# Filter work moved in a fused Fourier-mixing and SwiGLU kernel: additions behind both products, negations into the next step

## The chip, the cores and the metric

The kernel runs on one core of a Trainium2 chip. The metric is the device time of one execution in microseconds (us). Before the change four runs took 2838.94 to 2840.62 us, with a median of 2839.59 us. One more execution, which the hardware profiler recorded, took 2840.11 us; the span from its first to its last instruction is 2838.3 us.

## What is computed

```python
X = np.fft.rfft(x, axis=1)               # x: 8 batches, 3008 tokens, 256 channels
Y = X * (filt_r + 1j * filt_i)[None]     # one complex filter for all batches
y = np.fft.irfft(Y, n=3008, axis=1)
t = y.reshape(8 * 3008, 256)
g = t @ w_gate                           # 256 -> 1536
out = (g * (1 / (1 + np.exp(-g))) * (t @ w_val)) @ w_out     # 1536 -> 256
```

All of it is in float32.

## The kernel before

**Stages.** The Fourier transform of 3008 = 47 x 64 points is done as small matrix products in several stages with DRAM between them, and the two-layer network behind it uses products saved by algebra: four blocks of the input are combined into sums, so that fewer products are needed and the results are put together by additions. A batch goes through the network in 12 steps: 4 chunks of tokens (k) by 3 groups of hidden columns (g), step = 3k + g. While batch b is in the network, the transform of batch b+1 is done in pieces between its matmuls: steps 0 to 3 hold the first transform stage ("quads", L679), steps 4 to 10 the middle stages ("fours", L739), and the last stage (stage3, L919) is spread over several steps. Batch 0's transform is a prologue of about 78 us, batch 1's is done in batch 0's steps by other code, and batch 7's steps have no next transform.

**The order is written by hand.** SCHEDULE (L87 to L95) is a list of tokens that every step is issued from (loop at L1382), and pin() keeps each engine's instructions in that order. A token is one piece of work on one or two engines. Q, P, A, B and E are products on TensorE (L1034), W are the products with w_out (L1131). On ScalarE are f (negated copy of a product, L1049), c (copy, L1053), m (L1069), g and u (SiLU, L1076), and those s and e whose pair is listed with an x or a y token (L1060, L1065): they fill a PSUM bank from SBUF before a product adds to it. On VectorE are x and y, the other s and e, which fill a bank directly (L1056, L333 is the helper that records most of these), l (L329), h and v (L1081), o (L326) and z (L1102). On GpSimd are D (L1051, recorded at L329), S (sums of hidden tiles, L1085) and n (combined inputs of the next chunk). A prime marks work of the step before. A t token goes on with a last-stage piece. A b token, of which there are eight in a step (b0 to b7), goes on with the quads or the fours.

**Fours.** Step 4 + w handles part w of the filter (w = 0 to 5). Its generator yields seven times: at b0 the matmuls, b1 to b3 the evictions and the product of the transform with the real part of the filter (L779), b4 a DMA that swaps real and imaginary rows into tile q. At b5 VectorE multiplies the first half of q by the imaginary part (L818) and GpSimd adds it to y (L820, recorded at L326); at b6 the same for the second half; at b7 the filter's tile is given back and part w+1 is loaded. All these tiles are slices of one tile, lent. The products of step 5 + w's b0 read y.

**The filter.** The fours read the filter from one prepared array in DRAM (f_dram). Batch 1 builds it in its steps 0 to 2, at the tokens in FILTER_AT (L102; the code at L1413). At f1, P0, Q2 and h0 a DMA copies a piece of a filter from DRAM to DRAM (keep_filter). For the rows that need a minus sign, negated_filter(w, stage) works on one sixth of the imaginary filter: stage 0 is four DMAs into SBUF (L318), stage 1 a multiplication by -1 on ScalarE (L321, 64 x 1024), stage 2 one DMA out (L323). A step does two sixths: stage 0 at c1 and g0, stage 1 at u13 and E23, stage 2 at u01 and n1. Even sixths use one slice of lent, odd ones another.

**Queues.** Almost all DMAs are issued by SyncE's queue (SP), in program order; ScalarE issues the stores of the quads' and fours' results (d<-lent) between its own work. wt_t is the network's weights, of which four pieces are loaded again in every step from batch 1 on (L477), t is the last stage's input (L668), lent<-in_x_dram the next batch's input (L621).

Of the kernel before, what the change touches and what calls it, by code (L numbers as in the profile page):

```python
# [88 lines left out]
t4.3' W1 i3 x4.o' S10' x03 S11' i4 s13 b3 x5.o' P1 i5 o1 b4 t0.2 P0 o2 i6 z0.o c1 i7 D01 A13 g1 c0  # L89
i8 S20' Q2 S21' g0 y01 m13 t1.0 h0 i9 f2 s01 W6 t1.1 h1 i10 x23 D02 P2 o6 D12 A01 i11 c2 B13 g2 n3'  # L90
m01 t0.3 S30' t1.2 x02 W7 S31' g13 y12 y02 B01 h13 o7 t1.3 t2.0 s02 s12 g01 h2 b5 Q3 t2.1 h01 e12
A02 y23 b6 W4 e02 y03 m02 g3 A12 o4 z2.o t2.2 E12 m12 B02 t2.3 l12 b7 E02 u12 e13 g02 t3.0 h3 s23
l02 B12 v12 E13 t3.1 h02 u02 A23 n2 l13 g12 v02 W5 s03 e23 h12 e01 m23 A03 o5 z3.o u13 E23 t3.2 m03
v13 E01 l23 e03 t3.3 t4.0 l01 u23 B23 v23 u01 t4.1 E03 n1 v01 g23 B03 l03 W3 h23 g03 u03 h03 v03
""".split()  # L95
# [3 lines left out]
S00 S01 W1 S20 S21 S10 S11 W5 o1 W2 o5 S30 S31 W6 o2 z0.o o6 W3 o3 z1.o x0.o x1.o x2.o x3.o x4.o  # L99
x5.o W7 q4 o7 z3.o W4 o4 z2.o X0.o X1.o X2.o X3.o X4.o X5.o  # L100
""".split()
FILTER_AT = ("f1", "P0", "Q2", "h0", "c1", "g0", "u13", "E23", "u01", "n1")  # L102
BLOCKS = (0, 1, 3, 2)
PAIRS = ((0, 1), (1, 2), (2, 3), (0, 2), (1, 3), (0, 3))
PAIRS_USED = ((1, 3), (0, 1), (0, 2), (1, 2), (2, 3), (0, 3))
# [98 lines left out]
def kernel(  # L204
# [10 lines left out]
    nc = tc.nc  # L215
# [97 lines left out]
    def negated_filter(w, stage):  # L313

        t = room_of("et"[w % 2])[0:64].rearrange("p (s c) -> p s c", c=C)
        if stage == 0:
            for q in range(4):
                pin(nc.sync.dma_start(out=t[16 * q:16 * q + 16],  # L318
                                      in_=filter_rows(1, q // 2, q % 2, 4 * w, 4)))
        elif stage == 1:  # L320
            pin(nc.scalar.mul(t, t, -1.0))  # L321
        else:
            pin(nc.sync.dma_start(out=f_pairs[:, 0, 1, 4 * w:4 * w + 4], in_=t))  # L323

    def add(eng, dst, a, b):
        return eng.tensor_tensor(out=dst, in0=a, in1=b, op=ALU.add)  # L326
# [254 lines left out]
    class Spectral:  # L581
# [157 lines left out]
        def fours(self, w):  # L739

            tb = self.tb.pop(w)
            home, there = [], []
            if w:
                home = [bank(f"qc_{self.b}_{w}_{e}") for e in range(2)]
                y = self.p.pop(w - 1)
                for s in (0, 2, 1, 3):
                    for e in range(2):
                        r = slice(64 * e, 64 * e + 64)
                        pin(nc.tensor.matmul(  # L749
                            out=home[e][s // 2 * 64:s // 2 * 64 + 64, s % 2 * C:s % 2 * C + C],  # L750
                            lhsT=tb[r, 1, 64 * s:64 * s + 64], rhs=y[r, s],
                            start=s % 2 == 0, stop=True, skip_group_check=True))
            if w < N_FOUR:
                t = self.t2.pop(w)
                there = [bank(f"qb_{self.b}_{w}_{p}") for p in range(2)]
                for s in range(2):
                    for e in range(2):
                        for p in range(2):
                            r = slice(64 * p, 64 * p + 64)
                            a = 64 * (2 * s + e)  # L760
                            pin(nc.tensor.matmul(  # L761
                                out=there[p][64 * e:64 * e + 64, ts(s, C)],
                                lhsT=tb[r, 0, a:a + 64], rhs=t[r, s, e],
                                start=s == 0, stop=True, skip_group_check=True))
            yield
            z = y = None
            raw = []
            if w < N_FOUR:
                y = self.p[w] = room_of("y").rearrange("p (s c) -> p s c", c=C)
                there = [t.rearrange("p (s c) -> p s c", c=C) for t in there]  # L770

            def keep(p):
                t = t1pool.tile([128, NV, C], FP32, name=f"raw_{self.b}_{w}_{p}", tag="t1", bufs=2)
                raw.append(t)
                pin(nc.scalar.copy(out=t, in_=there[p]))

            def real(p):
                a = slice(2 * p, 2 * p + 2)
                pin(nc.vector.tensor_tensor(out=y[:, a], in0=there[p], in1=self.f[w][:, 0, a],  # L779
                                            op=ALU.mult))  # L780

            if home:
                z = room_of("g").rearrange("p (h f) -> p h f", h=2)
                pin(nc.scalar.copy(out=z[:, 0], in_=home[0]))
                pin(sub(nc.vector, z[:, 1], z[:, 0], home[1]))
            if there:
                keep(0)
            yield
            if home:
                pin(add(nc.vector, z[:, 0], z[:, 0], home[1]))  # L790
            if there:
                keep(1)
                real(0)
            yield
            if there:
                real(1)
            if home:
                rows = self.d2_tokens.rearrange("(h n) (r s) c -> (n r) h (s c)", h=2, r=2)
                for p in range(2):
                    at = (4 * w - 4 + 2 * p) * C  # L800
                    pin(nc.scalar.dma_start(out=rows[:, :, at:at + 2 * C],
                                            in_=z[64 * p:64 * p + 64]))
            yield
            q = None
            if there:
                q = room_of("e").rearrange("p (s c) -> p s c", c=C)
                for p in range(2):
                    pairs = [t.rearrange("(q r) s c -> q r s c", r=2)
                             for t in (q[:, 2 * p:2 * p + 2], raw[p])]
                    for r in range(2):  # L810
                        self.load(out=pairs[0][:, r], in_=pairs[1][:, 1 - r])
                self.load_four(w + 1)
            self.load_turns(w + 1)
            yield
            for half in range(2):
                a = slice(2 * half, 2 * half + 2)
                if there:
                    pin(nc.vector.tensor_tensor(out=q[:, a], in0=q[:, a], in1=self.f[w][:, 1, a],  # L818
                                                op=ALU.mult))
                    pin(add(nc.gpsimd, y[:, a], y[:, a], q[:, a]))  # L820
                yield
            if there:
                self.f.pop(w)
            self.load_filter(w + 1)
# [336 lines left out]
    with tc.tile_pool(name="start", bufs=1) as spool0:  # L1161
# [12 lines left out]
        n = 0  # L1174
# [154 lines left out]
    for b in range(B):  # L1329
# [35 lines left out]
        for step in range(NCHUNK * NG + (b == B - 1)):  # L1365
# [16 lines left out]
            for place, token in enumerate(SCHEDULE):  # L1382
                if b == 0 and this and place * TICKS % len(SCHEDULE) < TICKS and \
                        (step or place > SCHEDULE.index("A01")):
                    preparation.tick(step)
                old = token.endswith("'")
                op = token.rstrip("'")
                if op[0] == "i":
                    if older is not None and older.b == 0:
                        older.project(op)  # L1390
                elif op[0] == "t":
                    n = int(op[1])
                    ps = pieces_before if old else pieces
                    if n < len(ps):
                        next(ps[n], None)
                elif op[0] == "b":
                    next(bursts[step] if this else gap, None)
                elif op[0] in "Wo" or op.endswith(".o"):

                    g0 = older if old else before  # L1400
                    if g0 is not None and (old or not ghost):
                        g0.project(op)
                else:
                    g0 = before if old else this
                    if g0 is not None and not (ghost and op[0] == "S"):
                        g0.step(op)
                if old or this is None:
                    continue
                if b == 0 and (step, op) == (5, "A23"):
                    nxt.load_two(0)  # L1410
                if b + 2 < B and (step, op) in ((11, "Q2"), (11, "B01")):
                    following.load_x(int(op == "B01"))
                if b == 1 and step < 3 and op in FILTER_AT:  # L1413
                    n = FILTER_AT.index(op)
                    if n < 4:
                        keep_filter(4 * step + n)
                    else:
                        negated_filter(2 * step + n % 2, n // 2 - 2)
                if b and chunk and op == "B01":
                    cur.load_t4(chunk, 1)  # L1420
                for i in range(2):
                    if nxt and (step, op) == (10, ("A12", "E23")[i] if b else "E23"):
                        nxt.load_t4(0, i)
                for f, args in chores.get((step, op), ()) if b == 0 else ():
                    f(*args)
                if op in ends and not last and (b or step >= NT * NG - 1):
                    reload_weights((g + 1) % NG, ends[op])
# [34 lines left out]
```

## Time and profile before

| | |
|---|---|
| profiled execution | 2840.11 us |
| its span | 2838.3 us |
| median of four runs | 2839.59 us |
| matmuls busy | 2789.4 us, 98% of the span |
| weight loads busy | 2316.3 us, 82% |
| VectorE, ScalarE, GpSimd busy | 72%, 55%, 54% |
| negations L321 | 6, 1046 to 1057 ns each, from 474.8 to 536.6 us |
| products L818 | 72, 678 to 1603 ns each, median 865 ns |
| additions of 128 x 512 on GpSimd | 84, mean 1273 ns |
| steps of batch 1 | begin at 451.33, 480.54, 510.65, 542.66 us, and so on |

A float32 matmul is two records here, and in full flow the starts of two 128 x 188 matmuls are 159 ns apart although each is listed with some 322 ns, so busy shares of TensorE overlap. In a group's line the number behind the bar is busy time and mean duration, and then the idle time of the engine ahead of these instructions with what ended it. A timeline line gives start, duration, engine, source line, operation and count; what is in square brackets is the idle time before it and its releaser. A step begins where its first product (Q0, wk) does.

### The profile page before, as it was taken

How to read it: one execution, taken by the hardware profiler on the slowest of the kernel's cores; microseconds unless marked ns; L12 is line 12 of the kernel's file. 1: busy time of each engine (PE TensorE's matmuls, PEld its weight loads, DVE VectorE, ACT ScalarE, POOL GpSimd, SP SyncE). 2: the span in 40 equal slices, each digit the busy share in tenths (PEclk: the TensorE clock that was granted, in tenths of full speed). 3: DMA queues.
4: the chain of work that ended last, by engine and by line, in shares of the span. 5: the costliest groups of instructions: out<-in, count | busy, mean ns of one | idle time of the engine just before them, and what ended most of it. 6: DMA issues, size and time to landing. Idle time of an engine off the chain costs nothing.

```text
span 2838.3 us, 48561 instructions
## 1 busy us (share of the span) xinstructions
PE 2789.4 (98%) x15432; PEld 2316.3 (82%) x15432; DVE 2034.2 (72%) x4603; ACT 1566.7 (55%) x4202; POOL 1525.1 (54%) x1671
## 2 busy tenths in 40 slices
PE   8999999999999999999999999999999999999998
PEld 6777878788888888888888888878888888888887
DVE  6898766677667777677767677667776767766666
ACT  6775445555555555555555555555555555555554
POOL 4886566454545554455543555444554454545543
PEclk9999999999999999999999999999999999999999
DMA  9687867877666775667666676667765677645443
GB/s 231 221 269 250 274 204 226 271 222 231 189 186 203 246 219 177 199 212 235 218 182 199 212 237 205 188 190 233 229 204 177 214 221 227 195 146 153 151 137 82
DMA packets 363372, 586.58 MB, mean 207 GB/s; under 512 B 198388, under 2 KB 246260, under 8 KB 363024
## 3 DMA queue, kind: packets, MB, share of 16 engines
q1 hardware_dynamic: 337922, 534.73, 60.1%
q10 hardware_dynamic: 23406, 45.43, 5.9%
q0 software_dynamic: 1792, 3.34, 0.5%
q8 instruction: 125, 2.05, 0.3%
q14 instruction: 127, 1.04, 0.1%
HBM read 467.87 MB, written 101.34 MB: 201 GB/s over the span
## 4 chain that ended last, share of the span: by engine, by line
PE 86%; DVE 4%; POOL 3%; issue 2%; DMA 1%; ACT 0%; SPq 0%; POOLq 0%; DVEq 0%; ACTq 0%
PE wa L1034 23%; PE wk L1034 16%; PE wA L1131 16%; PE we L1034 12%; PE wG L1131 8%; PE wF L1131 4%; PE pd L937 3%; PE wqa L690 2%; PE wqc L749 1%; PE wqb L761 1%; DMA lent<-in_filt_i_dram 1%; DVE lent L818 1%; DVE y L333 1%; POOL out_dram L1116 1%; POOL h L329 0%
## 5 line engine op out<-in xcount | busy, mean ns | idle before, releaser
L1034 PE MATMUL wa<-y_t,wt_t 128*128 128x188 f32 x4464 | 880.9, 323 | 6.1 <-DVE wa L1056 2.0
L1034 PEld LDWEIGHTS wa<-y_t,wt_t 128*128 128x128 f32 x4464 | 747.1, 190 | 84.1 <-ACT wa L1060 11.0
L1034 PEld LDWEIGHTS wk<-y,wt_t 128*128 128x128 f32 x2976 | 494.7, 190 | 106.1 <-issue 33.4
L1034 PE MATMUL wk<-y,wt_t 128*128 128x188 f32 x2976 | 571.3, 325 | 0.0
L329 POOL TENSOR_TENSOR h<-h 128x376 f32<-128x376 f32 x572 | 557.9, 998 | 15.4 <-DVE h L326 15.2
L326 POOL TENSOR_TENSOR h<-h 128x376 f32<-128x376 f32 x190 | 183.6, 987 | 708.8 <-DVE h L1081 708.8
L1131 PE MATMUL wA<-h,wo_t 128*128 128x376 f32 x1532 | 551.3, 482 | 4.2 <-DVE o L326 4.1
L1034 PE MATMUL we<-y_t,wt_t 128*128 128x188 f32 x2232 | 435.2, 324 | 8.0 <-DVE we L333 4.1
L329 POOL TENSOR_TENSOR D<-f,f 128x376 f32<-128x376 f32 x288 | 280.0, 987 | 254.9 <-ACT f L1049 254.8
L329 DVE TENSOR_TENSOR we<-we,m 128x376 f32<-128x376 f32 x576 | 318.6, 554 | 121.5 <-PE we L1034 63.8
L1034 PEld LDWEIGHTS we<-y_t,wt_t 128*128 128x128 f32 x2232 | 369.3, 190 | 13.9 <-DVE we L333 8.2
L1131 PEld LDWEIGHTS wA<-h,wo_t 128*128 128x128 f32 x1532 | 274.8, 190 | 114.8 <-issue 11.1
L1069 ACT COPY m<-wa 128x376 f32<-128x376 f32 x576 | 272.8, 474 | 85.6 <-PE wa L1034 82.6
L333 DVE SCALAR_TENSOR_TENSOR y<-wk,c 128x376 f32<-128x376 f32 x480 | 246.3, 539 | 57.4 <-ACT c L1053 36.0
L1076 ACT ACTIVATE g<-wa 128x188 f32<-128x188 f32 x576 | 187.9, 326 | 165.1 <-PE wa L1034 154.9
L1131 PE MATMUL wG<-h,wo_t 128*128 128x376 f32 x768 | 274.3, 480 | 0.0
L1076 ACT ACTIVATE u<-we 128x188 f32<-128x188 f32 x576 | 188.3, 328 | 153.9 <-DVE we L329 147.7
L1053 ACT COPY c<-wk 128x376 f32<-128x376 f32 x288 | 136.4, 474 | 224.8 <-PE wk L1034 200.7
L1049 ACT ACTIVATE f<-wk 128x376 f32<-128x376 f32 x288 | 140.5, 488 | 174.0 <-PE wk L1034 142.2
L1065 ACT COPY we<-y 128x376 f32<-128x376 f32 x480 | 221.8, 480 | 18.4 <-DVE h L1081 13.7
L1081 DVE TENSOR_TENSOR h<-wa,g 128x188 f32<-128x188 f32 x576 | 198.6, 345 | 33.7 <-ACT g L1076 33.5
L1081 DVE TENSOR_TENSOR h<-we,u 128x188 f32<-128x188 f32 x576 | 197.4, 344 | 30.8 <-ACT u L1076 20.0
(162 smaller groups left out, 3516.7 us busy)
## 6 DMA issues: line engine op xcount, KB each, us to landing
wt_t<-w_all SPq DMA_DIRECT2D x174, 896.0 KB, 4.7
wt_t<-w_all SPq DMA_DIRECT2D x174, 768.0 KB, 4.4
lent<-filter SPq DMA_DIRECT2D x36, 1024.0 KB, 6.8
lent<-d SPq DMA_DIRECT2D x84, 256.0 KB, 4.2
d<-lent ACTq DMA_DIRECT2D x84, 256.0 KB, 3.8
d<-lent ACTq DMA_DIRECT2D x96, 192.0 KB, 3.0
lent<-raw SPq DMA_DIRECT2D x144, 128.0 KB, 2.1
t<-d SPq DMA_DIRECT2D x112, 128.0 KB, 4.4
```

Of the source, the lines that this page charges most:

```text
L326: return eng.tensor_tensor(out=dst, in0=a, in1=b, op=ALU.add)
L329: return eng.tensor_tensor(out=dst, in0=a, in1=b, op=ALU.subtract)
L333: return nc.vector.scalar_tensor_tensor(out=dst, in0=a, scalar=-1.0, in1=b, op0=ALU.mult, op1=ALU.subtract)
L937: pin(nc.tensor.matmul(out=rows, lhsT=self.t4[k, i][:, j, ts(cb, 128)], rhs=cols, start=j == 0, stop=True, skip_group_check=True))
L1034: pin(nc.tensor.matmul(out=ps[:, z], lhsT=self.wt[:, SLOT[p], z], rhs=rhs, start=start and z == 0, stop=True, skip_group_check=True))
L1049: pin(act.mul(self.small(f"f{i}", f"f{i}", 1), t[f"k{i}"], -1.0))
L1053: pin(act.copy(out=self.small(f"c{i}", f"c{i}", 1), in_=t[f"k{i}"]))
L1065: pin(act.copy(out=self.bank(f"e{at}"), in_=t[f"y{at}"]))
L1069: pin(act.copy(out=self.small(f"m{at}", "m", 4), in_=t[f"a{at}"]))
L1076: pin(act.activation(out=self.small(op, "g", 3, 1)[:, 0], in_=ps[:, 1], func=AF.Silu))
L1081: pin(v.tensor_tensor(out=dst, in0=ps[:, 0], in1=g, op=ALU.mult))
L1131: pin(nc.tensor.matmul(out=self.tiles[at], lhsT=wo_t[:, JB * q + i, WO[p], :], rhs=self.hs[i][:, HID[p]], start=start and i == 0, stop=Tru ...
```

## The change

The token b6 is put behind W4 and e02. In the fours, both additions on GpSimd are issued at b7 behind both products. Of the filter's preparation, stage 0 goes from c1 and g0 to g3 and A12, stage 1 to Q0 and P1 of the following step, stage 2 to c1 and h1 of the following step; so batch 1's step 3 is used as well. The copies at f1, P0, Q2 and h0 stay.

```diff
 (SCHEDULE)
-A02 y23 b6 W4 e02 y03 m02 g3 A12 o4 z2.o t2.2 E12 m12 B02 t2.3 l12 b7 E02 u12 e13 g02 t3.0 h3 s23
+A02 y23 W4 e02 b6 y03 m02 g3 A12 o4 z2.o t2.2 E12 m12 B02 t2.3 l12 b7 E02 u12 e13 g02 t3.0 h3 s23
...
-FILTER_AT = ("f1", "P0", "Q2", "h0", "c1", "g0", "u13", "E23", "u01", "n1")
+FILTER_AT = ("f1", "P0", "Q2", "h0", "g3", "A12", "Q0", "P1", "c1", "h1")
...
                 if there:
                     pin(nc.vector.tensor_tensor(out=q[:, a], in0=q[:, a], in1=self.f[w][:, 1, a],
                                                 op=ALU.mult))
-                    pin(add(nc.gpsimd, y[:, a], y[:, a], q[:, a]))
                 yield
+            for half in range(2 if there else 0):
+                a = slice(2 * half, 2 * half + 2)
+                pin(add(nc.gpsimd, y[:, a], y[:, a], q[:, a]))
             if there:
                 self.f.pop(w)
             self.load_filter(w + 1)
...
-                if b == 1 and step < 3 and op in FILTER_AT:
+                if b == 1 and step < 4 and op in FILTER_AT:
                     n = FILTER_AT.index(op)
-                    if n < 4:
+                    if n < 4 and step < 3:
                         keep_filter(4 * step + n)
-                    else:
-                        negated_filter(2 * step + n % 2, n // 2 - 2)
+                    elif 4 <= n < 6 and step < 3:
+                        negated_filter(2 * step + n % 2, 0)
+                    elif n >= 6 and step:
+                        negated_filter(2 * step - 2 + n % 2, n // 2 - 2)
```

## Prediction

> **What bounds the kernel.** I began with the page: shares, then the chain that ended last.
>
> ```profile
> PE 2789.4 (98%) x15432; PEld 2316.3 (82%) x15432; DVE 2034.2 (72%) x4603; ACT 1566.7 (55%) x4202; POOL 1525.1 (54%) x1671
> ...
> PE 86%; DVE 4%; POOL 3%; issue 2%; DMA 1%; ACT 0%; SPq 0%; POOLq 0%; DVEq 0%; ACTq 0%
> ```
>
> TensorE is the bound, so work elsewhere counts only where a matmul starts late. To find such places I cut the profile into steps. The first three rows are batch 1's steps 0 to 2, the last three batch 2's (step length, then busy time and count of PE, PEld, DVE, ACT, POOL, then granted clock, DMA share, GB/s).
>
> ```profile
> 451.33:480.54 29.21, 29.21 (x161) 23.89 (x160) 21.43 (x49) 16.94 (x44) 12.31 (x15) 1.00 0.85 276
> 480.54:510.65 30.11, 29.74 (x162) 23.84 (x160) 18.73 (x44) 18.18 (x45) 18.48 (x25) 1.00 0.89 287
> 510.65:542.66 32.01, 29.48 (x149) 23.66 (x148) 19.76 (x45) 16.73 (x42) 17.74 (x18) 0.95 0.79 243
> ...
> 798.06:827.27 29.21, 29.21 (x162) 23.89 (x160) 21.42 (x49) 15.46 (x42) 12.31 (x15) 1.00 0.64 198
> 827.27:856.48 29.21, 29.21 (x162) 23.89 (x161) 18.86 (x44) 16.42 (x43) 10.62 (x13) 1.00 0.71 198
> 856.48:884.08 27.60, 27.60 (x149) 22.23 (x148) 19.64 (x45) 14.77 (x40) 17.29 (x18) 1.00 0.67 210
> ```
>
> Steps of one number run the same matmuls. Batch 1's are 0, 0.90 and 4.40 us longer, and each has two ScalarE instructions more: the negations. The timeline of ScalarE at the end of step 2 shows them, and TensorE's what they hold up.
>
> ```profile
> 534.08 0.33 ACT L1076 ACTIVATE u<-we 128x188 f32<-128x188 f32 x1
> 534.30 1.05 ACT L321 ACTIVATE lent<-lent 64x1024 f32<-64x1024 f32 x1
> 536.58 1.06 ACT L321 ACTIVATE lent<-lent 64x1024 f32<-64x1024 f32 x1 [1.23 <-DMA lent<-in_filt_i_dram]
> 537.54 0.45 ACT L1069 COPY m<-wa 128x376 f32<-128x376 f32 x1
> 537.89 0.47 ACT L1065 COPY we<-y 128x376 f32<-128x376 f32 x1
> ```
>
> ```profile
> 535.08 0.80 PE L1034 MATMUL wa<-y_t,wt_t 128*128 128x188 f32 x4
> 538.41 1.62 PE L1034 MATMUL we<-y_t,wt_t 128*128 128x188 f32 x4 [2.53 <-ACT we L1065]
> 539.83 1.46 PE L1034 MATMUL wa<-y_t,wt_t 128*128 128x188 f32 x4
> ```
>
> The fill of the bank for E03 (e03, we<-y) stands behind two negations and a wait for their load. TensorE idles, then runs matmuls 0.31 us apart instead of 0.16.
>
> For the middle steps I took the late starts that repeat. Twice a batch, in steps 6 and 9 of batches 1 to 6, E13 waits for VectorE:
>
> ```profile
> 644.51 1.31 DVE L818 TENSOR_TENSOR lent<-lent 128x512 f32<-128x512 f32 x1
> ...
> 646.77 0.58 DVE L1102 STREAM_TRANSPOSE o<-o 128x384 f32<-128x384 f32 x1
> ...
> 647.71 0.55 DVE L333 SCALAR_TENSOR_TENSOR we<-wk,c 128x376 f32<-128x376 f32 x1
> ```
>
> ```profile
> 648.31 0.90 PE L1034 MATMUL we<-y_t,wt_t 128*128 128x188 f32 x4 [0.34 <-DVE we L333]
> ```
>
> It starts 0.51 us late and the next matmul 0.10 us: 12 x 0.61 = 7.3 us. That is what the first half of the change could be after.
>
> **What the Trainium skill says.** "SBUF — State Buffer", "Who interferes with whom": a VectorE instruction with two SBUF inputs contends with a GpSimd one that reads SBUF. The trace agrees: L818 takes 0.68 us at best, but 1.31 us beside a GpSimd addition (644.00 to 645.27). "TensorE: Matmul & The Clock Gate", "What's actually happening": an idle TensorE falls to half clock and gets it back after some busy time; here the nine matmuls after the idle stretch are twice as far apart, and the step's clock is 0.95. "Perfetto Trace Analysis", "Sequencer Loop": an engine's instructions wait in line for semaphores, so what stands behind a waiting one waits too, as the copy at 537.54 does.
>
> **Part 1: b6 and the additions.** Only an engine's own order counts. Between b6's old and new place the schedule has W4 (TensorE) and e02, whose pair has a y token, so it is a ScalarE copy. Neither is on VectorE, and the second product stays between y23 and y03. Between b5 and b7 no token has GpSimd work (no S, D or n). The two additions stay neighbours in the same place, each waiting for its own half's product as before. Comparing the two built programs instruction by instruction on each engine, I find VectorE, GpSimd and TensorE in the same order throughout, and the additions' waits unchanged. Removed 0, added 0: the 12 late starts stay. If a nearer overlap were meant, it would need an order that has not changed. The wait of GpSimd in these steps is nobody's critical wait either way.
>
> **Part 2: taking the negations from the ends of steps.** Step 0: its length equals batch 2's, so nothing comes back. Step 1: E03 at 508.01 is 0.50 us late behind two negations and restarts 0.10 us late: 0.60 us. The other 0.30 us of its 0.90 is at 496.44, A02 waiting for x02, D02 and so for GpSimd behind sixteen output DMAs of batch 0; it stays. Step 2: the four wa from 535.08 end their turn at 535.72 (4 x 0.159), the next matmul starts at 538.41, 2.70 us late; from there eight at 0.159 and one at 0.316 us would bring the second wG at 540.00, and it starts at 541.71, 1.70 us later for half clock. 4.40 us, all of the excess. What comes next when they go is TensorE itself, as batch 2's rows show. Sum: -5.00 us.
>
> **Part 3: their new places.** Stage 1 of the first sixth comes ahead of f0 in the next step. There ScalarE idles 1.36, 1.41 and 1.68 us (steps 1, 2, 3), waiting for wk0; 1.05 us fits. At P1 the other stands between the second and third of four d<-lent issues, with c1 behind. In step 3's times it would run 548.65 to 549.70, and two issues of 0.4 us put c1 at 550.5 instead of 550.14. Idle stretches of 0.17 and 1.42 us follow, so f2 is some 0.2 us late, against 0.58 us between its end and P2. Step 1 has an o copy there, late by 0.2 us with 2.7 us to spare. Cost taken: 0; bounds 0 to 0.3 us for each of three. A gain beyond Part 2 is excluded, as no matmul waits there.
>
> SP's queue: stage 0 of both sixths (8 loads) goes behind the h0 copy, a piece of wt_t and the four t loads; these move forward and the next two wt_t pieces back. They lose at most 4 us and land 9 us ahead of use. An issue also waits until the DMA eight before it has landed: the third t load at 535.45 waited for the wt_t load of 527.53, landed 535.43. From step 1 on, the loads also wait for the stores out of the same slice, 5.3 to 7.1 us each. Step 0's loads land by about 477, before 480. Step 1's first sixth: store issued about 496, landed 502, loads issued by 504, landed 508.5 (3.6 to 5.7 us each); ScalarE asks at 509.5 (its last u of step 1 ends at 510.13, less the 0.6). Step 2's: the x loads end at 524, as before; filter copies, stores and wt_t follow at some 0.6 us each, the stores at about 525.5 and 528; then four t loads. The first sixth's last load has the second store as its eighth before: 528 + 6.2 (median landing of these stores), so it is issued about 534.5 and, with 4.6 us, landed at 539.2 (538 to 540.5). With 5.0 us taken out, ScalarE asks at 536.9 (541.87 less 5.0) and f0 would start at 538.6 (543.56 less 5.0). So this negation waits, f0 ends near 540.8, and the copies of wqa behind it are due at 540.8. TensorE has 0.7 to 0.9 us after these copies. Cost: 0 if landed by 540.0, then 1 us per us; bounds 0 to 1 us, taken 0.2. Stage 2's stores and the next load into the slice land by 564, with the first use at 567. Cost 0.
>
> **Sum.** Against the profile: 2838.3 - 5.0 + 0.2 = 2833.5 us of span, plus 1.8 around it, 2835.3. The median of the runs is 0.5 us under the profiled execution: 2834.8 us, or -0.17%.
>
> **Rivals.** (a) A late load: the last sixth lands at 541 to 542 and costs 1 to 2 us: 2836.3. For it: the queue of eight and the wt_t landings of 6.3 to 7.9 us. Against: every wait in my chain is at its median. (b) Slower than before: the same load behind f0 in step 3, much later. Past 540.0 each us idles TensorE one us, and beyond some 2.5 us the half clock adds 1.7. From a landing at 543.3 the 5.0 us are gone; at 545 the time is 2834.6 + 5 + 1.7 = 2841.3. It needs the chain to slip 6 us. (c) Another wait ends E03 in step 2 and only half comes back: 2837. Against: batch 2's step has the same order without the negations and no late start. (d) The additions do leave VectorE's way and the 12 starts are in time: 2834.8 - 7.3 = 2827.5. Only the 1.31 us speaks for it; the unchanged order speaks against.
>
> **Chances.** Forecast 0.70, (a) 0.16, (b) 0.05, (c) 0.05, (d) 0.04. A measurement of this kernel can tell about 0.2% from no change, 5.7 us, so 2833.9 is the line. The forecast stays above it unless the unprofiled late start is 0.9 us longer: I give that 0.12 of its 0.70. Faster 0.12 + 0.04 = 0.16; slower needs 2845.3, 0.02; within 0.82. The range 2833.6 to 2838.0 reaches from the forecast less noise over (a) to the end of (c); out are (b), (d) and about 0.06 below.
>
> **What would show it.** Right: steps 1 and 2 of batch 1 last 29.5 and 27.6 us; E13 in steps 6 and 9 still waits for L333, 0.51 us late; L818 keeps 1.31 us beside the addition; the third step's first negation starts after 538. Wrong: a late start near 540 (a, b), or VectorE's L818 shorter in steps 6 and 9 (d).

## The result, and the profile after

The changed kernel takes 2836.66 us (median of 42 runs, 2833.88 to 2839.26), the kernel before, run beside it, 2839.54 us (60 runs, 2836.26 to 2847.34). The ratio is 0.9989, 95% interval 0.9984 to 0.9993: 2.9 us less, which counts as no change by the 0.2% of the prediction. The profiled execution of the changed kernel took 2834.54 us with a span of 2832.8 us, 5.5 us under the span before. So the two profiles differ by nearly twice as much as the medians, and that gap is what most experiments below are about.

Below the changed lines, line numbers are 2 higher than before (products L1036, products with w_out L1133). The page's shares are nearly those of before:

```profile
PE 2786.4 (98%) x15432; PEld 2313.8 (82%) x15432; DVE 2032.2 (72%) x4603; ACT 1566.0 (55%) x4202; POOL 1524.7 (54%) x1671
...
PE 85%; DVE 4%; POOL 3%; issue 2%; DMA 1%; ACT 0%; SPq 0%; POOLq 0%; DVEq 0%
```

The stretches of batch 1's steps 0 to 3 of the changed kernel (columns as in the prediction):

```profile
450.96:480.17 29.21, 29.21 (x162) 23.88 (x160) 21.41 (x49) 15.98 (x43) 12.31 (x15) 1.00 0.78 254
480.17:509.66 29.49, 29.34 (x161) 23.89 (x160) 18.73 (x44) 18.40 (x46) 18.45 (x25) 1.00 0.82 255
509.66:537.13 27.47, 27.47 (x149) 22.26 (x148) 19.73 (x45) 16.41 (x42) 17.29 (x18) 1.00 0.85 278
537.13:564.60 27.47, 27.47 (x149) 22.30 (x148) 21.03 (x48) 16.46 (x42) 12.37 (x15) 1.00 0.93 314
```

Steps 1 and 2 are 0.62 and 4.54 us shorter than before and step 3 is 0.14 us shorter. With step 0 unchanged that is 5.3 us of the 5.5 us. The DMA share of step 3 is 0.93; this will matter. ScalarE at the end of step 2 and the start of step 3:

```profile
536.07 0.33 ACT L1078 ACTIVATE g<-wa 128x188 f32<-128x188 f32 x1 [0.78 <-PE wa L1036]
536.29 0.32 ACT L1078 ACTIVATE u<-we 128x188 f32<-128x188 f32 x1
538.95 1.06 ACT L321 ACTIVATE lent<-lent 64x1024 f32<-64x1024 f32 x1 [2.34 <-DMA lent<-in_filt_i_dram]
539.92 0.46 ACT L1051 ACTIVATE f<-wk 128x376 f32<-128x376 f32 x1
```

No negation stands in the last part of the step any more. The next step's first one waits for its load and starts at 538.95; the prediction said after 538, with 539.2 as the landing.

The middle steps are as they were. VectorE and TensorE in step 6 of batch 1 of the changed kernel:

```profile
638.87 1.31 DVE L818 TENSOR_TENSOR lent<-lent 128x512 f32<-128x512 f32 x1
...
641.13 0.58 DVE L1104 STREAM_TRANSPOSE o<-o 128x384 f32<-128x384 f32 x1
...
642.06 0.55 DVE L333 SCALAR_TENSOR_TENSOR we<-wk,c 128x376 f32<-128x376 f32 x1
```

```profile
642.67 0.90 PE L1036 MATMUL we<-y_t,wt_t 128*128 128x188 f32 x4 [0.35 <-DVE we L333]
```

The second product still takes 1.31 us, and E13 is still 0.51 us late, in steps 6 and 9 of all six batches.

### The profile page after: what moved, and what is told of

It is laid out like the page before. It is cut to its first block, busy times and chain, and to the rows that moved or that the text cites. A ratio compares the mean times of both kernels' runs of the same rounds, so it can differ in the third digit from the quotient of the medians.

```text
span 2832.8 us, 48560 instructions
## 1 busy us (share of the span) xinstructions
PE 2786.4 (98%) x15432; PEld 2313.8 (82%) x15432; DVE 2032.2 (72%) x4603; ACT 1566.0 (55%) x4202; POOL 1524.7 (54%) x1671
## 3 DMA queue, kind: packets, MB, share of 16 engines
q14 instruction: 128, 1.05, 0.1%
## 4 chain that ended last, share of the span: by engine, by line
PE 85%; DVE 4%; POOL 3%; issue 2%; DMA 1%; ACT 0%; SPq 0%; POOLq 0%; DVEq 0%
PE wa L1036 22%; PE wk L1036 16%; PE wA L1133 16%; PE we L1036 12%; PE wG L1133 8%; PE wF L1133 4%; PE pd L939 3%; PE wqa L690 2%; PE wqc L749 1%; PE wqb L761 1%; DMA lent<-later_tbl 1%; POOL out_dram L1118 1%; POOL h L329 1%; DVE y L333 1%; DVE lent L818 1%
## 5 line engine op out<-in xcount | busy, mean ns | idle before, releaser
L1036 PE MATMUL wa<-y_t,wt_t 128*128 128x188 f32 x4464 | 879.5, 323 | 5.1 <-DVE wa L1058 1.3
L1036 PEld LDWEIGHTS wa<-y_t,wt_t 128*128 128x128 f32 x4464 | 746.1, 190 | 83.5 <-ACT wa L1062 11.1
L1036 PEld LDWEIGHTS wk<-y,wt_t 128*128 128x128 f32 x2976 | 494.6, 190 | 106.1 <-issue 33.4
L1036 PE MATMUL wk<-y,wt_t 128*128 128x188 f32 x2976 | 571.2, 325 | 0.0
L1133 PE MATMUL wA<-h,wo_t 128*128 128x376 f32 x1532 | 552.5, 483 | 4.5 <-DVE o L326 4.4
L1036 PE MATMUL we<-y_t,wt_t 128*128 128x188 f32 x2232 | 433.6, 323 | 5.1 <-DVE we L333 4.1
L1036 PEld LDWEIGHTS we<-y_t,wt_t 128*128 128x128 f32 x2232 | 368.2, 190 | 10.4 <-DVE we L333 8.3
L1133 PEld LDWEIGHTS wA<-h,wo_t 128*128 128x128 f32 x1532 | 275.4, 190 | 115.1 <-issue 11.3
L1133 PE MATMUL wG<-h,wo_t 128*128 128x376 f32 x768 | 273.9, 479 | 0.0
```

The costliest lines, as they stand in the source:

```text
L1036: pin(nc.tensor.matmul(out=ps[:, z], lhsT=self.wt[:, SLOT[p], z], rhs=rhs, start=start and z == 0, stop=True, skip_group_check=True))
L1133: pin(nc.tensor.matmul(out=self.tiles[at], lhsT=wo_t[:, JB * q + i, WO[p], :], rhs=self.hs[i][:, HID[p]], start=start and i == 0, stop=Tru ...
```

## Experiments

Times of variants are medians, ratios are to the kernel before with their 95% intervals. "Steps 0 to 3" are those of batch 1. By "placed as before" and "moved" I mean the negations with their loads and stores.

### The two halves of the change, each alone

The additions and b6 alone (the schedule line and the fours of the diff above, without FILTER_AT and the code that reads it):

> The kernel before with the first half of the change alone (first product with the filter moved behind W4 and e02 in the order, both GpSimd additions written behind the second product). My theory: this half moves nothing, since the first addition still waits for the first product alone; the time is that of the kernel before (2839.5 us, ratio 1.000), the second product L818 still takes 1.31 us beside the addition, E13 still starts 0.51 us late in steps 6 and 9 of batches 1 to 6, and steps 0 to 3 of batch 1 last 29.2, 30.1, 32.0 and 27.6 us. Rival (this half brings part of the gain): 1 to 3 us below the kernel before. What the second profile of the same steps adds: if the 2.70 us late start at the end of step 2 of batch 1 is smaller here, the gain of 5.5 us that the first two profiles show is partly luck of the one profiled execution.

Measured: 2838.25 us, ratio 0.9999 (0.9991 to 1.0007). L818 takes 1.30 us or more 24 times of 72, as before, and E13 is 0.51 us late at the same 12 places. This half does nothing. Its profile is a second one of the old placement, and there steps 1 and 2 last 30.56 and 30.34 us (30.11 and 32.01 in the first). E03's start at the end of step 2 is 2.64 us late, but no half clock follows.

The filter's moves alone (FILTER_AT and its code, without the rest):

> The changed kernel without the first half of the change: only the negations, their loads and their stores are moved. My theory: all of the gain, 2836.7 us (ratio 0.9989 to the kernel before), and steps 0 to 3 of batch 1 last 29.2, 29.5, 27.5 and 27.5 us. Rival (the additions matter): 2838 to 2839.5 us. Rival (late load): the first negation of step 3 starts later than in the first profile of the change (at its start plus some us) and step 3 or step 2 is longer than 27.5 us by what it is late beyond 1 us.

Measured: 2836.53 us, ratio 0.9991 (0.9985 to 0.9998): the whole gain of the change. But the execution that was profiled took longer (span 2838.0 us): step 3 lasts 31.35 us, not 27.5. The load was not the reason: the negation that waits for it starts 0.64 us into the step and makes no matmul late. What held ScalarE was the last of four d<-lent issues, in a view of ScalarE in step 3 of this variant (ACTq lines are issues of DMAs; here two are merged in a line):

```profile
543.32 0.78 ACTq L707 DMA_DIRECT2D d<-lent  x2
544.28 1.06 ACT L321 ACTIVATE lent<-lent 64x1024 f32<-64x1024 f32 x1 [0.80 <-DVE lent L329]
544.64 3.75 ACTq L707 DMA_DIRECT2D d<-lent  x2
548.43 0.47 ACT L1053 COPY c<-wk 128x376 f32<-128x376 f32 x1 [3.09 <-PE wA L1131]
...
549.95 0.54 ACT L1049 ACTIVATE f<-wk 128x376 f32<-128x376 f32 x1
```

```profile
550.54 0.91 PE L1034 MATMUL wk<-y,wt_t 128*128 128x188 f32 x4 [1.93 <-ACT f L1049]
```

The second pair of issues takes 3.75 us instead of 0.79 us: the third issue 0.31, the fourth 3.42 us. The view names TensorE as what ended ScalarE's idle time at 548.43, but the product that this copy reads had been done by then for almost 3 us; it is the issue that ended. Six pieces of work behind it, f2 the last, are late, TensorE starts 2.09 us late, and half clock adds the rest. No issue of SyncE is listed between 541.26 and 549.52 us, so ScalarE's issue was not waiting its turn behind one of those.

### Why an issue on ScalarE takes 3 us

The queue of SyncE shows what has moved besides the loads. First the kernel before (step 3 starts at 542.66), then the changed kernel (537.13):

```profile
532.26 4.38 SPq L596 DMA_DIRECT2D t<-d  x4
536.74 0.84 SPq L477 DMA_DIRECT2D wt_t<-w_all  x2
537.68 1.12 SPq L323 DMA_DIRECT2D filter<-lent  x2
541.42 0.33 SPq L477 DMA_DIRECT2D wt_t<-w_all  x1
```

```profile
531.15 7.61 SPq L318 DMA_DIRECT2D lent<-in_filt_i_dram  x8
538.86 1.61 SPq L477 DMA_DIRECT2D wt_t<-w_all  x3
540.64 0.54 SPq L323 DMA_DIRECT2D filter<-lent  x1
```

Before, two weight loads are issued 5.9 and 5.4 us ahead of the step and the third 1.2 us ahead. Now the eight loads of the third pair of sixths stand in front of them, waiting one by one for older DMAs, and the weights follow 1.7 to 3.0 us into the step: 0.9 + 0.8 + 0.8 MB. At some 400 GB/s (the rate of that stretch in the trace) they fill the DMA engines up to 8 or 9 us into the step, and 5 to 7 us into it ScalarE issues its four. A further profile and time of the changed kernel:

> The changed kernel as it is, once more, for a further profile of it and a time beside the variants. Three profiles of kernels with the moved negations so far: the last of the four d<-lent issues on ScalarE in step 3 of batch 1 took 0.45, 3.42 and 1.64 us, and step 3 lasted 27.5, 31.4 and 27.9 us. Theory (these issues are held up by the transfers of the moved loads, and that is where the gain goes in part of the executions): 2836.7 us, the issue again over 1 us or, where it isn't, a time in the fast part of its runs. Rival (one odd execution): the issue takes 0.45 us and step 3 lasts 27.5 us.

Measured: 2836.81 us, ratio 0.9988 (0.9981 to 0.9995). The issue took 0.61 us in its profile, and step 3 lasted 28.57 us: this time the load came 3.1 us after the step's start and a copy of wqa behind it was 0.41 us late for TensorE; another late start, of 0.50 us, waits for GpSimd.

The same, counted from each trace in step 3: when the first packet of ScalarE's own queue (q10) starts after its first issue, how long the fourth issue takes, and how long steps 0 to 3 last together. The variant short_negation, in the order of the kernel before, is described further below.

| kernel | first q10 packet, us | fourth issue, us | steps 0 to 3, us |
|---|---|---|---|
| placed as before: before, add_only, swap_before | 0.81, 0.82, 0.81 | 0.44, 0.48, 0.44 | 118.93, 117.72, 120.12 |
| placed as before: short_negation | 0.96 | 0.63 | 117.25 |
| moved: after, filter_only, again | 3.63, 3.51, 3.56 | 0.45, 3.42, 0.61 | 113.64, 117.53, 114.79 |
| moved: adds_behind_both, adds_again | 3.60, 3.36 | 1.64, 3.14 | 114.04, 115.57 |
| no_third_load | 0.81 | 0.44 | 113.77 |

(adds_behind_both, adds_again and swap_before change the additions, which lie in later steps.) With the moved placement ScalarE's queue gets nothing moved for 3.4 to 3.6 us, while 1.3 to 1.4 MB of SyncE's queue go first; with the old placement it starts within 1 us. In short_negation the third weight load is issued 1.4 us into the step and 0.4 MB are still ahead: there the second issue takes 1.05 us and the fourth 0.63. So in step 3 the issues over 1 us lie where transfers of SyncE are still ahead of ScalarE's, but they are not slow each time. Elsewhere the traces, those of the old placement too, have single issues of d<-lent of up to 1.65 us; among all 96 in each of the 14 traces only the 3.42 and the 3.14 us stand out.

To take the cause away without moving anything else in the order, I left the third pair's loads out:

```diff
-                    elif 4 <= n < 6 and step < 3:
+                    elif 4 <= n < 6 and step < 2:
                         negated_filter(2 * step + n % 2, 0)
```

> The changed kernel without the eight loads of the third pair of blocks (end of step 2 of batch 1); their negations and stores stay and work on the second pair's blocks once more, so part of the filter is wrong: this part of the work is left out. In the changed kernel these loads stand ahead of three weight loads in SyncE's queue and push them from before step 3 to 1.7 us into it; the weights (2.5 MB) then keep the DMA engines busy while ScalarE issues d<-lent. Theory: without the loads the weight loads are issued before step 3 starts, the DMA engines are free when ScalarE issues (packets of its own queue start within 1 us of the first issue and not 3.5 us after it), the fourth issue takes 0.45 us, the first negation of step 3 starts within 0.3 us of the step, step 3 lasts 27.5 us, and the time is 1 to 1.5 us below the changed kernel, 2835.4 us. Rival (the weights are no cause; the queue of ScalarE is slow by itself in that step): the fourth issue still takes over 0.6 us in this profile and the time is that of the changed kernel.

Measured: 2836.0 us, ratio 0.9988 (0.9982 to 0.9995). ScalarE in step 3 of this variant:

```profile
544.28 0.78 ACTq L707 DMA_DIRECT2D d<-lent  x2
545.11 1.06 ACT L321 ACTIVATE lent<-lent 64x1024 f32<-64x1024 f32 x1 [0.67 <-DVE lent L329]
545.60 0.79 ACTq L707 DMA_DIRECT2D d<-lent  x2
546.57 0.47 ACT L1055 COPY c<-wk 128x376 f32<-128x376 f32 x1 [0.40 <-PE wk L1036]
```

The packets start within 0.8 us, the issues are short and step 3 lasts 27.61 us. One detail came out otherwise: only one weight load is issued ahead of the issues, the other two wait for a DMA of ScalarE and follow at 546.95 us. So the DMA engines were free because two of the weight loads came later still, not because all came earlier. The profile supports the cause; the time does not show a gain: the ratio is the 0.9988 that the changed kernel had beside the kernel before, with intervals that reach 0.06 to 0.07% (some 2 us) to either side, more than the 1 to 1.5 us expected. What the slow issue costs in an execution without a profile is therefore not shown.

### What the negations cost in their old place

> The kernel before with the six negations of ScalarE left out: the part of the filter that they negate keeps its sign; loads and stores stay where they are. It gives the most that any place of the negations can bring. My theory (the change takes the whole cost of the negations away): within 0.3 us of the changed kernel, that is 2836.5 us, steps 0 to 3 of batch 1 at 29.2, 29.5, 27.6 and 27.6 us. Rival (in most runs a late load in step 3 takes part of the gain back): 2 to 3 us below the changed kernel, about 2834.3 us.

Measured: 2849.73 us, ratio 1.0035 (1.0021 to 1.0048), 10 us slower. This upper bound failed. Leaving ScalarE's operation out changed what SyncE's weight loads wait for: at the end of step 0 they wait 12 us for ScalarE's d<-lent of step 1, and TensorE starts late for the weights, 5.1 us in step 1, 1.8 us at the start of step 3 and 3.3 us later in it. So I kept the operation and its waits and made it short:

```diff
-            pin(nc.scalar.mul(t, t, -1.0))
+            pin(nc.scalar.mul(t[:, 0, 0:1], t[:, 0, 0:1], -1.0))
```

> The kernel before with each of its six negations cut to one column of 1024 (the other columns keep their sign, so part of the work is left out); order, loads, stores and waits stay. It gives what the six negations cost in the old place. Theory: the late starts at the ends of steps 1 and 2 of batch 1 shrink to what the load of the second block makes late (the short operation still waits for it), at most 1.2 us; steps 0 to 3 last 29.2, 29.5, 27.6 to 28.8 and 27.6 us; about 3.5 to 4.5 us below the kernel before, 2835.3 us. Rival (the wait for the load and not the negation makes the late start of 2.7 us): half of it stays, 2837.5 us.

Measured: 2840.85 us, ratio 1.0000 (0.9992 to 1.0009): the 3.5 to 4.5 us expected are outside the interval, which leaves room for a gain of 2.3 us at most. ScalarE and TensorE at the end of its step 2:

```profile
537.96 0.20 ACT L321 ACTIVATE lent<-lent 64x1 f32<-64x1 f32 x1
540.64 0.20 ACT L321 ACTIVATE lent<-lent 64x1 f32<-64x1 f32 x1 [2.48 <-DMA lent<-in_filt_i_dram]
540.75 0.45 ACT L1069 COPY m<-wa 128x376 f32<-128x376 f32 x1
541.10 0.47 ACT L1065 COPY we<-y 128x376 f32<-128x376 f32 x1
```

```profile
541.62 0.91 PE L1034 MATMUL we<-y_t,wt_t 128*128 128x188 f32 x4 [2.08 <-ACT we L1065]
```

The two operations take 0.20 us each and E03 is still 2.24 us late. In this step the wait for the second sixth's load held up the bank's fill, and not the 2 us of work. In step 1 too the short operation waits 2.13 us for its load and E03 is 0.90 us late; in the kernel before, the two negations of step 1 ran one behind the other without such a wait, and E03 was 0.50 us late. Where these loads land differs between executions, and with it the loss: in the three profiles of the old placement with whole negations (before, add_only, swap_before), E03 was 0.50, 0.97 and 0.41 us late in step 1, and 2.70, 2.64 and 3.90 us in step 2.

### The additions out of VectorE's way

The first half of the change leaves the first addition waiting for the first product alone. One turned loop makes GpSimd's own queue wait for both:

```diff
-            for half in range(2 if there else 0):
+            for half in ((1, 0) if there else ()):
                 a = slice(2 * half, 2 * half + 2)
                 pin(add(nc.gpsimd, y[:, a], y[:, a], q[:, a]))
```

> The changed kernel with its two GpSimd additions in the other order (second half first), so that the queue of GpSimd waits for the second product before it adds anything. My theory: the second product L818 then has no addition beside it and takes 0.68 us instead of 1.31 us wherever it had one (24 of 36 times), E13 of steps 6 and 9 starts in time at 12 places of 0.61 us, and the time falls by 6 to 7 us below the changed kernel, to about 2830 us. Rival (VectorE is late for another reason, or the additions now lie beside other VectorE work and lengthen that): L818 is short, but less than 2 us are gained. Rival (the additions, 0.6 us later, delay the sums of GpSimd behind them): new late starts, same time or slower.

Measured: 2827.34 us, ratio 0.9957 (0.9945 to 0.9970), with this turn on top of the changed kernel: 9.2 us below filter_only, which ran beside it, where 6 to 7 us had been expected. Step 6 of batch 1, on GpSimd, VectorE and TensorE:

```profile
640.92 2.50 POOL L326 TENSOR_TENSOR lent<-lent 128x512 f32<-128x512 f32 x2 [2.00 <-PE wA L1133]
```

```profile
640.11 0.68 DVE L818 TENSOR_TENSOR lent<-lent 128x512 f32<-128x512 f32 x1
640.71 0.53 DVE L333 SCALAR_TENSOR_TENSOR y<-wk,c 128x376 f32<-128x376 f32 x1
641.17 0.53 DVE L326 TENSOR_TENSOR o<-o,wA 128x376 f32<-128x376 f32 x1
641.73 0.58 DVE L1104 STREAM_TRANSPOSE o<-o 128x384 f32<-128x384 f32 x1
642.23 0.53 DVE L329 TENSOR_TENSOR we<-we,m 128x376 f32<-128x376 f32 x1
642.67 0.55 DVE L333 SCALAR_TENSOR_TENSOR we<-wk,c 128x376 f32<-128x376 f32 x1
```

```profile
643.35 0.82 PE L1036 MATMUL we<-y_t,wt_t 128*128 128x188 f32 x4
```

The view puts GpSimd's wait down to TensorE, but the second product ends at 640.79 and the additions begin 0.13 us later. That product takes 0.68 us in place of 1.31, E13 starts without a wait, and what lies beside the additions now (641.17 to 642.67) takes as long as it did without them. The Trainium skill, "SBUF — State Buffer", "Who interferes with whom", says just that: a VectorE instruction with at most one input in SBUF, outside its two-port modes, does not contend with GpSimd. Over the whole kernel, groups L818 of the changed kernel and of this variant (the number behind the bar is busy time, then the mean):

```profile
L818 DVE TENSOR_TENSOR lent<-lent 128x512 f32<-128x512 f32 x72 | 69.1, 960 | 0.0
```

```profile
L818 DVE TENSOR_TENSOR lent<-lent 128x512 f32<-128x512 f32 x72 | 53.7, 745 | 0.0
```

Steps 5 to 9 are about 0.07, 0.64, 0.02, 0.07 and 0.66 us shorter in each of batches 1 to 6 (step 5 of batch 6 by 0.36), 9.1 us together; the 12 late starts of E13 are 7.3 us of it. Once more, beside the variant below:

> The changed kernel with the two additions in the other order, once more: a second profile and a time beside the variant with the weights first. Theory: 2827.3 us; step 3 of batch 1 lasts 27.5 to 31 us, with the fourth d<-lent issue over 0.45 us in this profile too where the weights are late; steps 6 and 9 of batches 1 to 6 last 27.63 us.

Measured: 2828.05 us, ratio 0.9959 (0.9946 to 0.9971). The fourth issue of step 3 takes 3.14 us here and the step lasts 29.39 us.

With the negations left where they were:

> The kernel before with the additions alone in the other order (behind both products; second half first); the negations stay in their old places. Theory (the two halves are independent): 9.3 us below the kernel before, ratio 0.9967, about 2830 us; steps 6 and 9 of batches 1 to 6 last 27.63 us; steps 0 to 3 of batch 1 together 117 to 119 us, as in the two profiles with the old places so far (118.9 and 117.7 us), against 113.6 to 117.5 us in the five with the new places. Rival (the additions only bring so much together with the moved negations): over 2833 us.

Measured: 2831.03 us, ratio 0.9963 (0.9950 to 0.9977): the additions alone bring 9 us, with or without the moved negations. Steps 0 to 3 last 120.12 us, somewhat above the range expected: E03 is 3.90 us late in step 2, with half clock behind it.

### Three tries at the loads

Four buffers, so that loads need not wait for stores, and loads issued at c1 and g0 as before the change (the second store at g0 too):

```diff
-        t = room_of("et"[w % 2])[0:64].rearrange("p (s c) -> p s c", c=C)
+        q = 64 * (w // 2 % 2)
+        t = room_of("et"[w % 2])[q:q + 64].rearrange("p (s c) -> p s c", c=C)
...
-FILTER_AT = ("f1", "P0", "Q2", "h0", "g3", "A12", "Q0", "P1", "c1", "h1")
+FILTER_AT = ("f1", "P0", "Q2", "h0", "Q0", "P1", "c1", "g0")
...
```

> The changed kernel, but the six blocks that are negated lie in four buffers instead of two (both partition halves of the same rooms), so that the loads of a step need not wait for the stores of the step before and are issued earlier (behind c1 and g0 instead of g3 and A12); negations and stores stay at the new places (the second store behind g0). Theory (the late loads fill the transfers when ScalarE issues d<-lent in step 3): the fourth issue of step 3 takes 0.45 us, the first negation of step 3 starts with its step and not 0.6 to 1.8 us into it, step 3 lasts 27.5 us, and the time falls 1 to 2 us below the changed kernel, to 2835 us. Rival (the stores or the weight loads hold the issue up): the issue is slow again and the time is that of the changed kernel. Rival (the loads now collide with something earlier): other late starts in steps 1 or 2.

> The variant with four buffers and, besides, the two GpSimd additions in the other order. Theory: both gains add up, 9 us for the additions and 1 to 2 us for the loads: 2826 us, ratio 0.9953 to the kernel before. Rival (the loads bring nothing): 2827.3 us, as the changed kernel with the additions in the other order.

Measured: 2847.4 us, ratio 1.0025 (1.0017 to 1.0034), and 2838.21 us, ratio 0.9994 (0.9988 to 1.0001): the additions bring their 9 us again, the loads cost over 10. SyncE and TensorE around the start of step 1 in the variant without the turned additions:

```profile
474.39 2.25 SPq L597 DMA_DIRECT2D t<-d  x4
488.49 3.34 SPq L478 DMA_DIRECT2D wt_t<-w_all  x3
```

```profile
496.94 1.59 PE L1037 MATMUL wk<-y,wt_t 128*128 128x188 f32 x4 [4.88 <-DMA wt_t<-w_all]
```

The eight early loads no longer stand between the t loads and the weights, so that in the built program another DMA is the eighth ahead of the weights: they now wait 11.8 us for a d<-lent DMA that ScalarE issues only at 485.83 us. In the changed kernel the same weights are issued from 475.35 us on. TensorE stands 5.0 us for them, and 3.7 us for other weights at 558.7 us.

The third pair's loads behind the weights, its negations later in step 3 (behind f2 and behind A02's fill), its stores behind them, with the additions turned:

```diff
+THIRD = (((2, "v03"), 4, 0), ((2, "v03"), 5, 0), ((3, "f2"), 4, 1), ((3, "s02"), 5, 1),
+         ((3, "s02"), 4, 2), ((3, "s02"), 5, 2))
...
+                for at, w, stage in THIRD if b == 1 else ():
+                    if (step, op) == at:
+                        negated_filter(w, stage)
...
```

> The changed kernel with the additions in the other order and with the third pair's loads moved behind the weight loads in SyncE's queue; its two negations follow later in step 3 (behind f2 and behind the copy for A02, idle places of 1.4 and 1.0 us), its stores behind the second. All work is done. Theory: the weights are early again, the fourth issue takes 0.45 us, step 3 lasts 27.5 us, and it is 1 to 1.5 us below the variant with the additions alone: about 2826 us, ratio 0.9955 to the kernel before. Rival (a load or a store, now later, is late for something in steps 3 or 4, such as the reload of the filter in step 3): step 3 or 4 longer than 27.6 or 29.8 us, same time or slower.

Measured: 2828.22 us, ratio 0.9958 (0.9945 to 0.9972), the same as with the turned additions alone. The weights come from 537.09 us on, 3.4 us ahead of step 3, the packets of ScalarE's queue start 0.8 us after the first issue and the issues are short, but the loads behind the weights wait for d<-lent in their turn:

```profile
537.09 2.60 SPq L479 DMA_DIRECT2D wt_t<-w_all  x3
548.85 4.09 SPq L320 DMA_DIRECT2D lent<-in_filt_i_dram  x8
```

```profile
552.93 1.06 ACT L323 ACTIVATE lent<-lent 64x1024 f32<-64x1024 f32 x1 [2.25 <-DMA lent<-in_filt_i_dram]
```

ScalarE waits 2.25 us for them in front of c2, and TensorE starts 1.40 us late at 555.5, so step 3 lasts 29.11 us. One wait has been traded for another.

## Why the prediction was nearly right

**The number.** Forecast 2834.8 us, measured 2836.66 us, inside the range; no change by the stated bound. The gain is 2.9 us where the working had 4.8; in the profiles, what is missing lies in Part 3.

**Part 1 (additions): right.** The half alone measures 0.9999, L818 and E13 are untouched. Rival (d) fell for this change. When the order really changes, 2827.3 and 2828.1 us are measured where (d) had 2827.5, but that is luck: (d) took 7.3 us from a time that was 1.9 us too low, and the turned additions bring about 9 us; the two misses cancel.

**Part 2 (what comes back): right for the profile it was made from.** It gave -5.0 us, and the profile after shows it: step 1 keeps 0.28 us of its 0.90, step 2 keeps none of its 4.40. A further 0.14 us in each of steps 1 to 3 had not been foreseen; in step 1 a longer wait at A02 (0.42 us with its restart, in place of 0.29) takes it back. In each of the three the first two products of W1 start 0.16 and 0.32 us after the product ahead of them, in place of 0.22 and 0.39; in the built program W1 takes over a bank that ScalarE frees, not a later one of VectorE. That this is the cause was not tried.

**The cause given in Part 2 was not divided.** It named two negations and a wait for their load and priced them together. The short negation shows that in step 2 the load is the larger part. A load's landing is not a constant: with the old placement and whole negations, steps 0 to 3 lasted 117.72, 118.93 and 120.12 us, and the profile that was read was one draw of these. Half clock after a late start is as uneven: the 1.7 us of it were not there at all in one draw of three.

**Part 3 failed in one term.** Of the two weight pieces that the loads push back it said that they "lose at most 4 us and land 9 us ahead of use", cost 0. Counted from the step that they run into, they lose 7.6 us (from 5.9 and 5.4 us ahead of step 3 to 1.7 and 2.2 us into it). No matmul waits for them; but they are late in another sense, since they fill the DMA engines when ScalarE issues d<-lent. For those the working had "two issues of 0.4 us". The prediction looked at who waits for the weights, not at who shares the engines with them. The measured price, in profiles: step 3 with the moved placement lasts 28.9 us on average over five, 1.5 us above the 27.47 us of the first, where the working had 0.2 us. Steps 0 to 3 last 113.64 to 117.53 us, 115.11 us on average; with the old placement it is 118.92 us over three, so 3.8 us stand beside 2.9 us in the medians (2.0 to 4.5 by the interval).

**The 5.5 us between the two first profiles** are then mostly a lucky draw on one side. The profiled execution before took 0.6 us more than its median, the profiled execution after 2.1 us less than its own; its steps 0 to 3 are the shortest of the five.

**Rival (a)** had the right step and the right size, 1 to 2 us in step 3, but the wrong mechanism; that its 2836.3 us lies so near the measured time is luck too. The load that it feared made TensorE 0.41 us late in one of five profiles and not in the others; the issue of ScalarE, which no rival named, cost 0.4, 1.9 and 3.9 us in three of five.

**Left open.** Why the fourth issue is slow in some executions and takes 0.45 us in others, although the packets start equally late, no run tells; nor does a time without a profile show what it costs. And batch 1's step 0 begins anywhere from 449.9 to 454.6 us in the profiles, though up to there all these kernels run the same program; this noise of batch 0 is as large as the effect and was not looked into.

**A version that beats both kernels** is the changed kernel with its additions turned: 2827.3 and 2828.1 us, 0.9957 and 0.9959 of the kernel before.

## What to carry to other kernels

Moving an instruction's text behind another engine's work does nothing if its waits stay the same; turning two queued additions round, so that the first one waits for the later input, moved the pair and brought three times what the change did. When a DMA is moved past others in a queue, count whose transfers will now share the engines with which issue, and not only who waits for which data. And when a stall ends with a load's landing, one profile gives one draw of it: take its size from several before building a forecast on it.

## What the runs showed of the hardware

- An engine that issues a DMA can be held by the issue itself. The same d<-lent issue on ScalarE in step 3 took 0.44 to 0.48 us with free DMA engines (before, add_only, swap_before, no_third_load) and 0.45 to 3.42 us behind 1.3 to 1.4 MB of SyncE's transfers (five profiles). The Trainium skill, "Perfetto Trace Analysis", "DMA Instruction — HWDGE (DVE, Sync)", says that the recorded time of such an instruction is the lock wait and the use of the descriptor generator, and that the sequencer is free only afterwards; how long that gets under load it does not say. Other issues of d<-lent took up to 1.65 us in these traces; longer ones, of 3.14 and 3.42 us, appear in step 3 with late weights only.
- ScalarE's queue did not at once share the engines with SyncE's backlog: its first packet started 3.4 to 3.6 us after its issue in all five profiles with late weights, 0.96 us after it with 0.4 MB ahead (short_negation) and 0.8 us with none or little. The Trainium skill, "DMA: Bandwidth & Descriptors", "Queues, rings and completion order", has the engines go round between the queues that have work, packet by packet; these traces don't show that for queues fed in this order.
- TensorE's half clock (matmuls 0.31 us apart in place of 0.16) followed late starts of 2.09, 2.70 and 3.90 us (filter_only, before, swap_before) and not those of 1.82, 2.24 and 2.64 us (adds_again, short_negation, add_only): in this range the length alone does not tell. It followed all six of 3.31 to 5.19 us (no_negation and the two variants with four buffers).
